# Range bounds on VectorE, grouped transposes and a new order of the first steps in a fused attention and ReGLU kernel

## The chip, the cores and the metric

The kernel runs on one core of one Trainium2 chip. The metric is the device time of one execution in microseconds, as the median of several runs. The engines that matter are TensorE (PE in the profile: matrix products and transposes, results in PSUM), VectorE (DVE), ScalarE (ACT: exponentials, ReLU, copies), GpSimd (POOL: masks, casts, and the issue of the DMAs that convert to bf16) and SyncE (SP: the issue of the other DMAs).

## What is computed

Causal attention with 16 beacon rows ahead of the sequence, then a gated feed-forward layer. B, H, S, Nb, D = 8, 8, 576, 16, 64; d_model = 512, d_ff = 1536, so 4608 tokens pass the second part.

```
k_all = concat([beacon_k, k], axis=2); v_all = concat([beacon_v, v], axis=2)
scores = (q @ k_all.T) / sqrt(D)            # beacon columns always visible
scores = where(causal, -1e9, scores)
a = exp(scores - scores.max(-1)); a /= a.sum(-1) + 1e-09
x = (a @ v_all), heads side by side         # 4608 x 512
out = (maximum(x @ w_gate, 0) * (x @ w_val)) @ w_out
```

## The kernel before

**Attention.** For each batch b the kernel holds `kT` and `qT` (d on the partitions, two heads in 128 partitions) and `v`. Scores are made transposed, keys on the partitions, in units: a unit is one PSUM tile `s` of two banks (L333, `Unit.qk`), one exponential on ScalarE into `e` (L341, `Unit.exp`) and, where the unit touches the diagonal, a mask on GpSimd (L349). The exponentials are not shifted by the row maximum. A chunk is a group g of four heads and a range of 240, 256 or 80 query columns (`CHUNKS`). When all units of a chunk are there, `Chunk.av` (L377) multiplies by v (`ab`) and by ones (`os`, the row sums); `invert` (L385) takes the reciprocal `r` of the sums on VectorE, `scale` (L390) writes `xT` = `ab` * `r`. The tiles `ab` and `os` have one buffer each; in batch 0 the chunks of group 1 take the two buffers of `f` instead.

**Range check.** Since no maximum is subtracted, `note` (L393 on) keeps track of r over all chunks: on GpSimd it turns "r below 1e-10" into 1e30 (`low`, L398) and adds r and `low` to a running sum `far` (L401, twice). Near the end VectorE reduces `far` (`rows_in_range`), a matmul counts the good rows, and a general path, not taken here, would run if a row were out of range. One note is kept back for the next step (`while len(notes) > 1`). The tile r has four buffers.

**Feed-forward.** Tokens are taken in tiles of 512 columns of `xT`. `Ffn.up` (L415 gate, ReLU on ScalarE L418, L421 value, product `hT` on VectorE L423) runs for each of the 12 blocks of d_ff; `Ffn.down` (L428) makes 128 rows of output, copied by ScalarE (L431) and stored by SP. Every PSUM result of this part is one of the two buffers of `f`.

**Order.** Everything is issued in the order of a step list, `plan`, and every engine runs its own instructions in that order. A step of a batch makes the scores of two units, does the `av`, `invert` of the chunks that came due, then some feed-forward groups (`mine`), with the `scale` behind the first of them, then the actions that were put at or behind this step (`at`, `after`), then notes. A batch has 7 steps. Batch 0 (steps 0 to 6) has no feed-forward work; four steps without attention (`ALONE`, 7 to 10) follow, then batch 1 (11 to 17), and from step 18 on the other batches. The third number of a plan entry is a quota of feed-forward work in us, kept as a credit (1.7 for an up, 2.6 for a down).

**Loading.** Batches 0 and 1 come as halves of 256 rows. Batch 0's are loaded in float32 by SP and cast on VectorE or ScalarE (`cast_half`), batch 1's are converted by GpSimd's DMA (`load_cast_half`, L267). `turn_half` (L273 on, transposes at L281, moves at L282) transposes a half on TensorE into a PSUM tile: 8 transposes, a move of these to `kT` or `qT`, 8 more, a second move. `turn_two` does this for the k and the q half with one `s` tile. The last 64 rows (`tails`) and the beacon rows go through `cast_rows` (L295) and `turn_rows` (L302, L303). The weights come by GpSimd's DMA (`load_w` L309, `load_wo` L314). Later batches are loaded by SP, cast on GpSimd (L246, L242) and transposed by DMA.

Of the kernel before, what the change touches and what calls it, by code (L numbers as in the profile page):

```python
# [153 lines left out]
def kernel(  # L154
# [12 lines left out]
    nc = tc.nc  # L167
# [26 lines left out]
    far = const.tile([P, 256], FP32, name="far")  # L194
    nc.gpsimd.memset(far, 0.0)
# [6 lines left out]
    nrm = main.enter_context(tc.tile_pool(name="nrm", bufs=4))  # L202
# [6 lines left out]
    class Batch:  # L209
# [60 lines left out]
        def turn_half(self, x, i, ps, moves):  # L270

            h = self.h.pop((x, i, "half"))
            dst, c0 = (self.qT, 0) if x == "q" else (self.kT, Nb)  # L273
            c0 += i * 256
            for g, move in enumerate(moves):
                js = slice(2 * g, 2 * g + 2)
                for r in range(2):
                    for j in (2 * g, 2 * g + 1):
                        for a in range(2):
                            c = ((2 * j + a) * 2 + r) * D  # L280
                            nc.tensor.transpose(ps[a * D:(a + 1) * D, j, r], h[:, c:c + D], ident)  # L281
                move(dst[:, js, c0:c0 + 256].rearrange("a j (p r) -> a j p r", r=2),  # L282
                     ps[:, js].rearrange("a j r p -> a j p r"))
# [70 lines left out]
    class Chunk:  # L354
# [39 lines left out]
        def note(self):  # L394

            n = CHUNKS[self.ci][1]
            low = nrm.tile([P, 256], FP32, name="low", bufs=1)
            nc.gpsimd.tensor_scalar(out=low[:, :n], in0=self.r[:, :n], scalar1=1e-10,  # L398
                                    scalar2=1e30, op0=ALU.is_lt, op1=ALU.mult)
            for x in (self.r, low):  # L400
                nc.gpsimd.tensor_tensor(out=far[:, :n], in0=far[:, :n], in1=x[:, :n], op=ALU.add)  # L401
# [38 lines left out]
    def rows_in_range():  # L440
        most = const.tile([P, 1], FP32, name="most")
        nc.vector.tensor_reduce(most, far, op=ALU.max, axis=AX.X)
        ok = const.tile([P, 1], BF16, name="ok")
        nc.vector.tensor_scalar(out=ok, in0=most, scalar1=1e10, scalar2=None, op0=ALU.is_le)
        return ok

    def count_rows(ok):
# [12 lines left out]
    plan = ([(0, i, 0.0) for i in range(STEPS)]  # L460
            + [(None, 0, 4.5)] * ALONE
            + [(1, i, 2.1) for i in range(STEPS)]
# [3 lines left out]
    with tc.manual_schedule():  # L466
# [7 lines left out]
        def at(step, action):  # L474
            later.setdefault(step, []).append(action)
# [7 lines left out]
        def load_rest(x):  # L483
            x.tails = [x.load_rows(k[x.b, :, 512:]), x.load_rows(q[x.b, :, 512:])]
            for t in range(NKT):
                x.load("v", t)
# [6 lines left out]
        ps = s_ps.tile([P, 2, NP, 2, P], BF16, name="s")  # L493
        first.cast_half("k", 0, dve)
        first.turn_half("k", 0, ps[:, 0], (dve, dve))
        first.cast_half("q", 0, act)
        first.turn_half("q", 0, ps[:, 1], (act, dve))
# [3 lines left out]
        def load_both(n0, n1):  # L501
            load_w(wg, moe_w_gate, n0, n1)
            load_w(wv, moe_w_val, n0, n1)

        def turn_two(x, i):
            ps = s_ps.tile([P, 2, NP, 2, P], BF16, name="s")
# [10 lines left out]
        later_half = {}  # L517

        def after(step, action):
            later_half.setdefault(step, []).append(action)  # L520
# [18 lines left out]
        after(5, lambda: second.load_cast_half("k", 1))  # L539
        after(5, lambda: second.load_cast_half("q", 1))  # L540
        after(6, lambda: load_wo(0, 6))
        after(6, lambda: load_wo(6, 12))
# [40 lines left out]
        for s, (b, i, quota) in enumerate(plan):  # L583
# [14 lines left out]
            for u in units:  # L598
                u.qk()
            if units:  # L600
                units[0].exp()
# [5 lines left out]
            mine = []  # L607
            while queue and credit > queue[0][1] / 2:
                mine.append(queue.pop(0))
                credit -= mine[-1][1]  # L610
# [24 lines left out]
            while len(notes) > 1:  # L635
                notes.pop(0)()
# [9 lines left out]
        for note in notes:  # L646
            note()
# [44 lines left out]
```

## Time and profile before

| | |
|---|---|
| median of 3 runs | 428.46 us (427.62 to 428.52) |
| profiled execution | 428.95 us, of which the span of its instructions is 427.2 us |
| TensorE busy | 388.0 us, 91% |
| VectorE busy | 175.1 us, 41% |
| ScalarE busy | 192.3 us, 45% |
| GpSimd busy | 218.5 us, 51% |
| mean granted TensorE clock | 0.97 |

The groups of the three lines of `note` on GpSimd hold 41.0, 28.3 and 28.3 us in 48 instructions each. A line of the timeline reads: start, duration, engine, source line, operation, output<-input with partitions x elements, count, and in brackets how long the engine had been idle and which instruction released it. A group line reads: line, engine, operation, output<-input, count | busy us, mean ns of one | idle time before. A line of the stages reads: stretch, its length, busy us (and instructions) of PE, PEld (TensorE's weight loads), DVE, ACT and POOL, mean granted TensorE clock, DMA share, GB/s.

### The profile page before, as it was taken

The page shows a single profiled execution, that of the slowest core. Times are in us where ns is not written, and L with a number is a line of the kernel's source. Part 1 is how long each engine was busy: PE and PEld are TensorE (multiplying, and loading weights), DVE is VectorE, ACT ScalarE, POOL GpSimd, SP SyncE. Part 2 cuts the span into 40 slices and gives each one's busy share as a digit, 9 for nine tenths or more (in the row PEclk, how much of TensorE's full clock was granted, in tenths as well). Part 3 has the DMA queues.
Part 4 walks back from the last instruction along what each step waited for, and adds up shares of the span by engine and source line. Part 5 has one row for each costly group of instructions (what it writes and reads, how often), then busy time and mean ns, then how long its engine had stood idle before and what let it go on. Part 6 is the DMA issues. An engine that isn't in the chain of part 4 may idle for free.

```text
span 427.2 us, 10264 instructions
## 1 busy us (share of the span) xinstructions
PE 388.0 (91%) x4265; PEld 189.2 (44%) x4265; DVE 175.1 (41%) x230; ACT 192.3 (45%) x267; POOL 218.5 (51%) x357
## 2 busy tenths in 40 slices
PE   2672877889999999999999999999999999999994
PEld 1342333445454545544554445444544454444441
DVE  2363243444454355434553455344534442411310
ACT  2561122564645465545545554555545533323221
POOL 1699810796658575756675576648551651000000
PEclk9997688899999999999999999999999999999999
DMA  8999994562993499359937993898110011001002
GB/s 216 194 211 196 187 187 80 112 117 74 203 185 60 134 205 171 69 131 204 168 60 152 191 161 57 175 195 144 46 69 0 5 51 49 2 25 74 2 26 79
DMA packets 146516, 49.85 MB, mean 117 GB/s; under 512 B 133152, under 2 KB 141856, under 8 KB 146464
## 3 DMA queue, kind: packets, MB, share of 16 engines
q1 hardware_dynamic: 137472, 43.37, 51.5%
q0 software_dynamic: 8992, 5.77, 9.3%
q8 instruction: 35, 0.57, 0.6%
q14 instruction: 17, 0.14, 0.1%
HBM read 38.27 MB, written 9.44 MB: 112 GB/s over the span
## 4 chain that ended last, share of the span: by engine, by line
PE 85%; POOL 7%; DVE 2%; DMA 2%; ACT 1%; SPq 1%; issue 1%; DVEq 0%; ACTq 0%; POOLq 0%
PE f L421 24%; PE f L415 24%; PE f L428 22%; PE ab L377 6%; PE s L333 6%; PE os L377 2%; POOL e L349 1%; DMA raw<-in_v_dram 1%; POOL wg L309 1%; POOL wv L309 1%; DMA wide<-in_k_dram 1%; POOL far L401 1%; POOL hwide L267 1%; POOL low L398 1%; POOL v L242 1%
## 5 line engine op out<-in xcount | busy, mean ns | idle before, releaser
L423 DVE TENSOR_TENSOR hT<-g,f 128x512 bf16<-128x512 f32 x108 | 74.2, 687 | 124.5 <-PE f L421 123.0
L341 ACT ACTIVATE e<-s 128x1024 bf16<-128x1024 f32 (+2 forms) x112 | 104.9, 964 | 25.8 <-PE s L333 25.0
L415 PE MATMUL f<-xT,wg 128*128 128x512 bf16 x432 | 115.5, 391 | 0.8 <-DVE r L385 0.8
L421 PE MATMUL f<-xT,wv 128*128 128x512 bf16 x432 | 113.1, 384 | 0.0
L418 ACT ACTIVATE g<-f 128x512 f32<-128x512 f32 x108 | 64.5, 597 | 108.0 <-PE f L415 107.9
L385 DVE RECIPROCAL r<-os 128x240 f32<-128x240 f32 (+2 forms) x45 | 61.1, 1358 | 90.9 <-PE os L377 86.7
L428 PE MATMUL f<-wo,hT 128*128 128x512 bf16 x432 | 97.3, 379 | 0.0
L349 POOL TENSOR_SCALAR_AFFINE_SELECT e<-e 128x512 bf16<-128x512 bf16 (+2 forms) x80 | 46.6, 593 | 94.2 <-ACT e L341 91.1
L421 PEld LDWEIGHTS <-wv 128*128 128x128 bf16 x432 | 42.6, 99 | 64.0 <-issue 22.9
L428 PEld LDWEIGHTS <-hT 128*128 128x128 bf16 x432 | 40.9, 98 | 48.7 <-issue 0.2
L415 PEld LDWEIGHTS <-wg 128*128 128x128 bf16 x432 | 40.2, 100 | 48.9 <-issue 5.0
L431 ACT COPY ob<-f 128x512 f32<-128x512 f32 x36 | 21.1, 585 | 75.6 <-PE f L428 63.4
L377 PE MATMUL ab<-e,v 128*32 128x80 bf16 (+4 forms) x1320 | 40.3, 236 | 6.4 <-POOL e L349 2.9
L246 POOL CAST half<-raw 128x512 bf16<-128x512 f32 (+2 forms) x60 | 35.8, 611 | 15.6 <-DMA raw<-in_k_dram 9.8
L398 POOL TENSOR_SCALAR low<-r 128x240 f32<-128x240 f32 (+2 forms) x48 | 41.0, 854 | 3.6
L333 PE MATMUL s<-qT,kT 64*128 64x80 bf16 (+3 forms) x704 | 36.7, 238 | 3.0 <-ACT e L341 2.2
L377 PEld LDWEIGHTS <-v 128*32 128x32 bf16 (+1 forms) x1408 | 27.4, 99 | 22.2 <-issue 11.7
L333 PEld LDWEIGHTS <-kT 64*128 64x128 bf16 x704 | 21.5, 98 | 26.6 <-issue 25.3
L242 POOL CAST v<-raw 128x512 bf16<-128x512 f32 (+1 forms) x40 | 25.5, 642 | 14.5 <-DMA raw<-in_v_dram 13.9
L377 PE MATMUL os<-e,ones 128*32 128x240 bf16 (+4 forms) x660 | 32.6, 234 | 0.0
L401 POOL TENSOR_TENSOR far<-far,low 128x240 f32<-128x240 f32 (+2 forms) x48 | 28.3, 589 | 3.8
L401 POOL TENSOR_TENSOR far<-far,r 128x240 f32<-128x240 f32 (+2 forms) x48 | 28.3, 590 | 3.1
(40 smaller groups left out, 111.7 us busy)
## 6 DMA issues: line engine op xcount, KB each, us to landing
out_dram<-ob SPq DMA_DIRECT2D x36, 256.0 KB, 2.4
raw<-in_v_dram SPq DMA_DIRECT2D x24, 256.0 KB, 5.0
raw<-in_q_dram SPq DMA_DIRECT2D x24, 256.0 KB, 5.0
raw<-in_k_dram SPq DMA_DIRECT2D x18, 256.0 KB, 4.3
raw<-in_v_dram SPq DMA_DIRECT2D x8, 224.0 KB, 5.3
wo<-in_moe_w_out_dram POOLq DMA_DIRECT2D x2, 768.0 KB, 11.6
raw<-in_k_dram SPq DMA_DIRECT2D x6, 224.0 KB, 4.5
raw<-in_v_dram SPq DMA_DIRECT2D x8, 160.0 KB, 4.3
```

Source lines behind the costliest of these rows:

```text
L333: nc.tensor.matmul(self.s[:, a, c + j * n:c + (j + 1) * n], self.batch.kT[rows, 2 * g + j, kt * P:(kt + 1) * P], self.batch.qT[rows, 2 * g ...
L341: nc.scalar.activation(e[:, :k * 4 * n].rearrange("p (k a x) -> p a k x", k=k, a=2), self.s[:, :, :k * 2 * n].rearrange("p a (k x) -> p a ...
L349: nc.gpsimd.affine_select(out=cols[:, :, :m], in_=cols[:, :, :m], pattern=[[0, 4], [1, m]], compare_op=ALU.is_ge, fill=0.0, base=base, cha ...
L377: nc.tensor.matmul(o[:, q0 - cq0:q0 - cq0 + n], w, e[:kr, 2 * (hh % 2) + hh // 2], start=(i == 0 and part != 1), stop=(i == self.last), sk ...
L385: nc.vector.reciprocal(self.r[:, :n], self.os[:, :n])
L398: nc.gpsimd.tensor_scalar(out=low[:, :n], in0=self.r[:, :n], scalar1=1e-10, scalar2=1e30, op0=ALU.is_lt, op1=ALU.mult)
L401: nc.gpsimd.tensor_tensor(out=far[:, :n], in0=far[:, :n], in1=x[:, :n], op=ALU.add)
L415: nc.tensor.matmul(g[:, :n], wg[:, ki, nf * P:(nf + 1) * P], x[:, ki], start=(ki == 0), stop=(ki == KM - 1))
L418: nc.scalar.activation(gs[:, :n], g[:, :n], AF.Relu)
L421: nc.tensor.matmul(u[:, :n], wv[:, ki, nf * P:(nf + 1) * P], x[:, ki], start=(ki == 0), stop=(ki == KM - 1))
L423: nc.vector.tensor_mul(self.h[:, nf, c0:c1], gs[:, :n], u[:, :n])
L428: nc.tensor.matmul(o, self.h[:, nf, ms * P:(ms + 1) * P], wo[:, nf, :], start=(nf == 0), stop=(nf == NF - 1))
```

## The change

1. `note` no longer runs on GpSimd: VectorE keeps two running tiles, `least` and `most`, by one `min` and one `max` with r (both operands float32 in SBUF). A note is issued at the end of its own step, none is kept back. The tile r has three buffers in place of four. `rows_in_range` compares both tiles and reduces.
2. `turn_half` issues all 16 transposes of a half, then its two moves. Each half now has a PSUM tile of its own: batch 0's are `f` tiles, batch 1's are two `s` tiles where there was one.
3. Batch 0: the k half 1 is turned after step 0, the q half 1 between the two score units of step 1 (`between`); the tails are cast on VectorE in step 1, where ScalarE cast them in step 0. SP loads the first three tiles of v ahead of the tails.
4. Later actions move by one step: the last weight columns from step 2 to 3, the halves of batch 1 from 4 and 5 to 5 and 6, `wo` from 6 to 7.
5. In `plan`, whole numbers now count feed-forward groups instead of microseconds: 0, 3, 3, 2 in the four steps alone and 1 in each step of batch 1.

```diff
-    far = const.tile([P, 256], FP32, name="far")
-    nc.gpsimd.memset(far, 0.0)
+    bounds = [const.tile([P, 256], FP32, name=n) for n in ("least", "most")]
+    for x in bounds:
+        nc.vector.memset(x, 1.0)
...
-    nrm = main.enter_context(tc.tile_pool(name="nrm", bufs=4))
+    nrm = main.enter_context(tc.tile_pool(name="nrm", bufs=3))
...
+            for j in range(NP):
+                for r in range(2):
+                    for a in range(2):
+                        c = ((2 * j + a) * 2 + r) * D
+                        nc.tensor.transpose(ps[a * D:(a + 1) * D, j, r], h[:, c:c + D], ident)
             for g, move in enumerate(moves):
                 js = slice(2 * g, 2 * g + 2)
-                for r in range(2):
-                    for j in (2 * g, 2 * g + 1):
-                        for a in range(2):
-                            c = ((2 * j + a) * 2 + r) * D
-                            nc.tensor.transpose(ps[a * D:(a + 1) * D, j, r], h[:, c:c + D], ident)
...
         def note(self):
             n = CHUNKS[self.ci][1]
-            low = nrm.tile([P, 256], FP32, name="low", bufs=1)
-            nc.gpsimd.tensor_scalar(out=low[:, :n], in0=self.r[:, :n], scalar1=1e-10,
-                                    scalar2=1e30, op0=ALU.is_lt, op1=ALU.mult)
-            for x in (self.r, low):
-                nc.gpsimd.tensor_tensor(out=far[:, :n], in0=far[:, :n], in1=x[:, :n], op=ALU.add)
+            for x, op in zip(bounds, (ALU.min, ALU.max)):
+                nc.vector.tensor_tensor(out=x[:, :n], in0=x[:, :n], in1=self.r[:, :n], op=op)
...
+        nc.vector.tensor_scalar(out=least, in0=least, scalar1=1e-10, scalar2=None, op0=ALU.is_ge)
+        nc.vector.scalar_tensor_tensor(out=least, in0=most, scalar=1e10, in1=least,
+                                       op0=ALU.is_le, op1=ALU.mult)
+        nc.vector.tensor_reduce(ok, least, op=ALU.min, axis=AX.X)
...
-            + [(None, 0, 4.5)] * ALONE
-            + [(1, i, 2.1) for i in range(STEPS)]
+            + [(None, 0, n) for n in (0, 3, 3, 2)]
+            + [(1, i, 1) for i in range(STEPS)]
...
         def turn_two(x, i):
-            ps = s_ps.tile([P, 2, NP, 2, P], BF16, name="s")
-            for y, n in enumerate("kq"):
-                x.turn_half(n, i, ps[:, y], (dve, act))
+            for n in "kq":
+                ps = s_ps.tile([P, 2, NP, 2, P], BF16, name="s")
+                x.turn_half(n, i, ps[:, 0], (dve, act))
...
+        after(0, lambda: first.turn_half("k", 1, f_half(), (dve, act)))
         after(0, lambda: first.cast_half("q", 1, dve))
-        after(0, lambda: turn_two(first, 1))
         after(0, lambda: first.cast("v", 1, pool))
-        after(0, lambda: cast_tails(first, act))
-        at(1, lambda: turn_tails(first))
+        between[1] = lambda: first.turn_half("q", 1, f_half(), (dve, act))
+        at(1, lambda: None)
+        at(1, lambda: cast_tails(first, dve))
+        after(1, lambda: turn_tails(first))
...
-        after(2, lambda: load_both(768, 1536))
         after(3, lambda: first.cast("v", 4, pool))
+        after(3, lambda: load_both(768, 1536))
         after(4, lambda: load_rest(second))
-        after(4, lambda: second.load_cast_half("k", 0))
-        after(4, lambda: second.load_cast_half("q", 0))
...
+        after(5, lambda: second.load_cast_half("k", 0))
+        after(5, lambda: second.load_cast_half("q", 0))
...
-            while len(notes) > 1:
+            while notes:
                 notes.pop(0)()
```

**What moves on VectorE in batch 0.** The chunks (group 0 or 1, columns 256 or 80) of batch 0 in VectorE's order; `os`/`ab` are group 0, `f` group 1. Before:

```order
L385 RECIPROCAL r<-os 128x256
L390 TENSOR_TENSOR xT<-ab,r 128x2x256
L385 RECIPROCAL r<-f 128x256
L390 TENSOR_TENSOR xT<-f,r 128x2x256
L385 RECIPROCAL r<-os 128x80
L390 TENSOR_TENSOR xT<-ab,r 128x2x80
```

The same chunks with the change:

```order
L386 RECIPROCAL r<-os 128x256
L391 TENSOR_TENSOR xT<-ab,r 128x2x256
L398 TENSOR_TENSOR least<-least,r 128x256
L398 TENSOR_TENSOR most<-most,r 128x256
L386 RECIPROCAL r<-f 128x256
L391 TENSOR_TENSOR xT<-f,r 128x2x256
L398 TENSOR_TENSOR least<-least,r 128x256
L398 TENSOR_TENSOR most<-most,r 128x256
L386 RECIPROCAL r<-os 128x80
L391 TENSOR_TENSOR xT<-ab,r 128x2x80
```

A `min` and a `max` now stand between a chunk's `xT` and the next chunk's reciprocal.

**What moves on GpSimd in batch 0**, steps 3 to 6: masks (AFFINE_SELECT), notes and DMA issues. Before:

```order
L398 TENSOR_SCALAR low<-r 128x240
L401 TENSOR_TENSOR far<-far,r 128x240
L401 TENSOR_TENSOR far<-far,low 128x240
L349 AFFINE_SELECT e<-e 128x4x128
L242 CAST v<-raw 80x512
L267 DMA hwide<-in_k_dram 128x8x128
L267 DMA hwide<-in_q_dram 128x8x128
L398 TENSOR_SCALAR low<-r 128x240
L401 TENSOR_TENSOR far<-far,r 128x240
L401 TENSOR_TENSOR far<-far,low 128x240
L349 AFFINE_SELECT e<-e 128x320
```

With the change:

```order
L350 AFFINE_SELECT e<-e 128x4x128
L243 CAST v<-raw 80x512
L310 DMA wg<-in_moe_w_gate_dram 128x2x768 x2
L310 DMA wv<-in_moe_w_val_dram 128x2x768 x2
L350 AFFINE_SELECT e<-e 128x320
L268 DMA hwide<-in_k_dram 128x8x128
L268 DMA hwide<-in_q_dram 128x8x128
L350 AFFINE_SELECT e<-e 128x320
```

The notes are gone ahead of each mask; the last weight columns are issued behind the mask of step 3, and the halves of batch 1 behind the first 320-wide mask.

**What moves on VectorE around the tails**, steps 1 and 2 of batch 0 (`half` 64x512 are the tails, `kT<-f` and `qT<-f` their moves). Before:

```order
L282 COPY qT<-s 128x2x256
L385 RECIPROCAL r<-os 128x240
L390 TENSOR_TENSOR xT<-ab,r 128x2x240
L303 COPY kT<-f 128x4x64
L303 COPY qT<-f 128x4x64
L385 RECIPROCAL r<-f 128x240
```

With the change:

```order
L283 COPY qT<-f 128x2x256
L386 RECIPROCAL r<-os 128x240
L391 TENSOR_TENSOR xT<-ab,r 128x2x240
L296 CAST half<-raw 64x512 x2
L304 COPY kT<-f 128x4x64
L304 COPY qT<-f 128x4x64
L398 TENSOR_TENSOR least<-least,r 128x240
L398 TENSOR_TENSOR most<-most,r 128x240
L386 RECIPROCAL r<-f 128x240
```

The casts of the tails stand on VectorE behind the first chunk's `xT`; on TensorE their transposes stand, as before, ahead of the scores of step 2.

More of the change, by code (lines that the diff above doesn't have):

```diff
@@ L440, in rows_in_range @@
     def rows_in_range():
[L441 to L442 removed]
+        least, most = bounds
         ok = const.tile([P, 1], BF16, name="ok")
[L444 removed]
+        nc.vector.tensor_scalar(out=least, in0=least, scalar1=1e-10, scalar2=None, op0=ALU.is_ge)
+        nc.vector.scalar_tensor_tensor(out=least, in0=most, scalar=1e10, in1=least,
+                                       op0=ALU.is_le, op1=ALU.mult)
+        nc.vector.tensor_reduce(ok, least, op=ALU.min, axis=AX.X)
         return ok
@@ L483, in load_rest @@
         def load_rest(x):
+            for t in range(3):
+                x.load("v", t)
             x.tails = [x.load_rows(k[x.b, :, 512:]), x.load_rows(q[x.b, :, 512:])]
-            for t in range(NKT):
+            for t in range(3, NKT):
                 x.load("v", t)
@@ L597 @@
                 units = [Unit(batches[b], order[2 * i + x]) for x in range(2)]
-            for u in units:
+            for j, u in enumerate(units):
                 u.qk()
+                if j == 0 and s in between:
+                    between[s]()
             if units:
```

23 lines of the change are left out of this document (12 added, 11 removed).

## The prediction

> **What bounds the kernel now.** I read the page's clock row first, then the busy times by stage, then the timeline of the stages where TensorE is not full.
>
> ```profile
> PEclk9997688899999999999999999999999999999999
> ```
>
> ```profile
> 30.00:44.40 14.40, 4.70 (x208) 3.77 (x209) 6.55 (x8) 3.13 (x4) 13.81 (x19) 0.72 1.35 199
> 44.40:56.40 12.00, 12.00 (x41) 4.54 (x41) 4.06 (x8) 2.98 (x5) 7.23 (x13) 0.76 1.31 199
> 56.40:61.70 5.30, 2.32 (x45) 1.73 (x44) 2.64 (x6) 0.59 (x1) 1.86 (x3) 0.87 0.87 165
> 61.70:69.90 8.20, 8.20 (x28) 2.98 (x28) 1.37 (x2) 2.38 (x4) 0.00 (x0) 0.67 0.88 157
> 69.90:75.30 5.40, 2.61 (x45) 1.65 (x44) 1.98 (x3) 1.73 (x3) 0.00 (x0) 0.88 0.00 0
> 75.30:103.10 27.80, 24.65 (x350) 12.51 (x348) 13.08 (x14) 15.14 (x20) 22.48 (x36) 0.96 0.52 100
> 103.10:421.00 317.90, 317.84 (x3338) 151.93 (x3337) 134.30 (x173) 151.17 (x213) 156.16 (x256) 1.00 0.52 104
> ```
>
> From 103.1 us TensorE is busy without a break at full clock (317.84 of 317.90). The change leaves its amount of work alone: eight ups in the four steps alone, four ups and three downs in batch 1, in both versions. So the time moves by what the first 103 us gain or lose, unless VectorE's new work opens gaps later. GpSimd is nearly full from 30 to 44.4 us (13.81 of 14.40) while TensorE has 4.70. The timeline shows who waits:
>
> ```profile
> 37.06 0.69 POOL L401 TENSOR_TENSOR far<-far,low 128x240 f32<-128x240 f32 x1
> 37.70 0.48 POOL L349 TENSOR_SCALAR_AFFINE_SELECT e<-e 128x320 bf16<-128x320 bf16 x1
> 38.23 0.32 PE L377 MATMUL ab<-e,v 80*32 80x80 bf16 x8 [2.88 <-POOL e L349]
> 41.98 0.72 POOL L401 TENSOR_TENSOR far<-far,low 128x256 f32<-128x256 f32 x1
> 42.66 0.47 POOL L349 TENSOR_SCALAR_AFFINE_SELECT e<-e 128x320 bf16<-128x320 bf16 x1
> 43.18 0.33 PE L377 MATMUL f<-e,v 80*32 80x80 bf16 x8 [3.76 <-POOL e L349]
> 44.40 1.86 PE L415 MATMUL f<-xT,wg 128*128 128x512 bf16 x4 [0.83 <-DVE r L385]
> ```
>
> Masks stand behind notes; TensorE waits 2.88 and 3.76 us for them, and the first up begins at 44.40. Later it waits inside the turns of batch 1's halves, each time for a move, before the next eight transposes:
>
> ```profile
> 57.60 0.41 PE L281 MATMUL s<-ident,hwide 128*64 128x128 bf16 x8
> 58.81 0.41 PE L281 MATMUL s<-ident,hwide 128*64 128x128 bf16 x8 [0.79 <-DVE kT L282]
> 61.16 0.64 PE L281 MATMUL s<-ident,hwide 128*64 128x128 bf16 x8 [0.85 <-DVE qT L282]
> 75.33 1.89 PE L415 MATMUL f<-xT,wg 128*128 128x512 bf16 x4
> ```
>
> After such gaps the clock is down: a group of four 512-column products takes twice as long.
>
> ```profile
> 46.27 1.71 PE f L421 x4
> 50.82 0.86 PE f L415 x4
> ```
>
> **The change, part by part.** Prices of one instruction in ns (after the bar: busy us, mean ns of one):
>
> ```profile
> L385 DVE RECIPROCAL r<-os 128x256 f32<-128x256 f32 x15 | 26.4, 1758 | 33.6 <-PE os L377 33.6
> L385 DVE RECIPROCAL r<-os 128x80 f32<-128x80 f32 x15 | 9.9, 658 | 26.4 <-PE os L377 26.4
> L390 DVE TENSOR_TENSOR xT<-ab,r 128x512 bf16<-128x512 f32 x15 | 10.3, 688 | 0.3
> L390 DVE TENSOR_TENSOR xT<-ab,r 128x160 bf16<-128x160 f32 x15 | 4.8, 322 | 0.3
> L401 POOL TENSOR_TENSOR far<-far,r 128x256 f32<-128x256 f32 x16 | 11.6, 726 | 1.0
> L349 POOL TENSOR_SCALAR_AFFINE_SELECT e<-e 128x512 bf16<-128x512 bf16 x48 | 29.7, 635 | 10.4 <-ACT e L341 7.3 <-DMA out_dram<-ob 1.7 <-DMA raw<-in_q_dram 0.7
> L282 DVE COPY kT<-s 128x512 bf16<-128x512 bf16 x5 | 3.4, 690 | 1.7 <-PE s L281 1.7
> L282 ACT COPY kT<-s 128x512 bf16<-128x512 bf16 x3 | 1.8, 585 | 6.6 <-PE s L281 6.6
> L295 DVE CAST half<-raw 64x512 bf16<-64x512 f32 x2 | 0.7, 407 | 0.0
> L195 POOL MEMSET far<- 128x256 f32 x1 | 0.3, 316 | 0.0
> L442 DVE TENSOR_REDUCE most<-far 128x1 f32<-128x256 f32 x1 | 0.4, 410 | 0.0
> ```
>
> No row shows min or max. VectorE's two-input rows grow by (688 - 322) / 352 = 1.04 ns an element, so 256 columns make 0.42 us and 80 make 0.24, a pair 0.84 and 0.48. One operand of those rows lies in PSUM, here both lie in SBUF; below, an instruction costs at least half (0.2), above, GpSimd's own row of that shape (0.73). I take 0.42, by VectorE's rows, which are the nearest.
>
> *Up to the first up.* I follow the chain in the new order from these rows.
>
> ```profile
> 18.94 1.87 ACT L341 ACTIVATE e<-s 128x960 bf16<-128x960 f32 x2
> 20.96 1.66 DVE L385 RECIPROCAL r<-os 128x240 f32<-128x240 f32 x1 [4.27 <-PE os L377]
> 21.91 1.94 ACT L341 ACTIVATE e<-s 128x1024 bf16<-128x1024 f32 x2 [1.10 <-PE s L333]
> 30.06 1.76 DVE L385 RECIPROCAL r<-os 128x256 f32<-128x256 f32 x1 [2.98 <-PE os L377]
> ```
>
> Step 1's exponentials start about 1.8 us earlier (near 17.1): two waits between transposes go, and ScalarE no longer casts the tails first. The first chunk's reciprocal follows at about 19.8, 1.2 earlier. Then part is given back: xT ends at 19.8 + 1.66 + 0.66 = 22.1, two tail casts of 0.41 follow on VectorE (22.9), and TensorE, whose order has the tails' transposes ahead of step 2's scores, waits for them: step 2's exponentials start at about 23.9, 2.0 late. ScalarE then runs without the gaps that it had, so that the reciprocal of the first 256-column chunk comes at about 30.5, 0.45 late. From there VectorE sets the pace: 30.5 + 1.76 + 0.69 + 0.84 = 33.8 for the first chunk with its pair, 1.76 + 0.69 for the second (36.25), which frees the `f` tile of the last chunk's av; the pair 0.84, the 80-column chunk 0.66 + 0.32 + 0.48, and the last one's 0.66 + 0.32 end at 39.5. The masks are no longer late: with no notes ahead of them, GpSimd's weight issues and hwide issues end before TensorE reaches them. On SP the tails now stand behind three tiles of v: they land later, but VectorE takes them only at 22.1, and the first tile of v comes sooner. One buffer less of r costs nothing, since VectorE alone now writes and reads it, in its own order. Hand-offs of 0.1 to 0.2 make it 39.7, so **-4.7 us**, with bounds of 2 (step 2 later, a pair at 1.46) and 6.5 (a pair at 0.4, no tail wait).
>
> *From the first up to the end of the eighth.* Before: 12.0 + 5.3 + 8.2 = 25.5. Now six ups come first: 12.0 for five with the clock down at first, as before, and 1.9 for the sixth. The small transposes take 1.2 (56.4 to 57.6), the two halves 4 x 0.41 = 1.6 without waits, because each has its own tile; the moves run under the seventh up. Two warm ups and a ReLU that stands behind ScalarE's moves: 3.8. Together 20.5, **-5.0 us**; of these 2.5 are the waits and 2.5 the slow clock of the sixth and seventh up in the row of 61.7 (0.67).
>
> *To the ninth up.* Before 5.4. Now 1.6 of transposes, and the first scores wait for their `s` tile: two moves 0.69 + 0.59 behind the k half, the same behind the q half on the same engines: 3.5, **-1.9 us**.
>
> *Batch 1.* Before 27.8, with 24.65 busy, of which the ninth up's slow start costs 0.9. The longest gap is this one, in a step that had no feed-forward group; now each step has one:
>
> ```profile
> 95.36 0.40 PE L377 MATMUL ab<-e,v 128*32 128x256 bf16 x8 [1.64 <-DVE xT L390]
> ```
>
> I take 2.0 of the 3.15 us idle and the 0.9: **-2.9 us** (between 1 and 4).
>
> *From batch 2 on.* 36 pairs on VectorE. Its room between two jobs there:
>
> ```profile
> 157.76 0.69 DVE L423 TENSOR_TENSOR hT<-g,f 128x512 bf16<-128x512 f32 x1 [1.69 <-PE f L421]
> 161.50 0.69 DVE L423 TENSOR_TENSOR hT<-g,f 128x512 bf16<-128x512 f32 x1 [1.18 <-PE f L421]
> 163.24 1.76 DVE L385 RECIPROCAL r<-os 128x256 f32<-128x256 f32 x1 [1.05 <-PE os L377]
> ```
>
> A pair stands behind the last hT of a step; the next job is idle for 1.05 us (a reciprocal) or 1.69 (an hT) before it, and 0.84 fits into either. The loop value product, hT, value product is tight, so whatever overruns costs TensorE at once; I charge 0.3 in all. The two memsets (316 ns on GpSimd) lie before the first load lands, 0.6 if they did not; the reduction at the end (410 now, two more instructions of about 0.4) fits into the 1.18 beside an hT, or costs 0.8.
>
> Sum: -4.7 - 5.0 - 1.9 - 2.9 + 0.3 = -14.2. The profiled execution took 428.95 (a span of 427.2 and 1.75 around it), 0.49 over the median: 414.75 for such an execution, 414.3 against the median of 428.46.
>
> **The rivals.** *The clock stays up before the first up* (gaps of 1 to 2 us in place of 2.88 and 3.76): three groups at 0.86 in place of 1.71 save 2.6 more, 411.7. Against it: VectorE's chain leaves TensorE little work from 34 to 39.7.
>
> *The clock falls in the turn.* 2.8 us of transposes in a row may count as idleness; the two ups behind them then run slow, +2.6, 416.9. For it: in the stage from 56.4 the clock fell with 45 short instructions in it (0.87 on the mean). Against it: half of that stage was waiting. The Trainium skill (TensorE: Matmul & The Clock Gate, Part 4) says that transposes do not count as activity for the clock; no run here shows dense transposes alone.
>
> *The data come too late.* The DMA moves 199 GB/s to 56.4 us, before as after, and the last weight columns, with `wo` and the halves of batch 1 behind them in GpSimd's queue, are issued a step later, some 3 us by my chain. The halves themselves no longer wait for notes there, and are needed only at about 55. If the columns or batch 1's halves are not there, the turn waits and the 4.7 are lost: 419.0.
>
> *Slower: VectorE's pairs hold TensorE in the long stage.* If each min and max waits for a running mask of 0.64, a pair takes 0.84 + 1.28 = 2.1, 1.05 over the room; at the half of the 36 pairs whose overrun meets a full-length reciprocal or hT that is 18 x 1.05 = 19, so 433. It turns the sign from 0.39 us a pair over all 36 on. Against it: GpSimd loses its notes and is idle more than half of that stage. The Trainium skill (SBUF — State Buffer, Who interferes with whom) speaks for it: a VectorE instruction with two SBUF inputs contends with a GpSimd instruction that reads SBUF. This trace has no such VectorE instruction.
>
> *No change*: the start is paced by loads altogether and the ups only wait elsewhere, 428.
>
> **How the numbers follow.** Forecast 0.50, clock up 0.18, clock falls 0.14, data late 0.10, VectorE slower 0.05, no change 0.03. A measurement of this kernel tells about 0.2% from none. Faster 0.92, same 0.03, slower 0.05. The range goes from 410.5 (clock up, and 1 of the bounds) to 420.0 (data late, and 1).
>
> **What would show it.** Right: first up at 39.7, the ninth at about 63.7, no wait of TensorE for a mask over 1 us, no wait between the transposes of a half, batch 2 at about 89, and a stage behind it of the same length. Wrong: a later first up with TensorE waiting for a DMA; min and max well over 0.42; gaps of TensorE in the long stage ahead of value products, with a min or max on VectorE just before the hT that they wait for.

## The result and the profile after

The changed kernel takes 411.56 us (median of 4 runs, 410.49 to 412.26) beside 428.49 for the kernel before on the same chip: a ratio of 0.9603, 95% interval 0.9571 to 0.9635. The forecast was 414.3, the range 410.5 to 420.0. The profiled execution took 410.93 us, of which the span is 408.7. By the ratio 17.0 us are gained. In a later set of runs the unedited kernel gave 0.9605 (0.9577 to 0.9633).

The clock row of the page of after, then its stages (columns as in the table of before; the second stretch begins with the first up, the last with batch 2):

```profile
PEclk9998999999999999999999999999999999999999
```

```profile
30.00:38.23 8.23, 4.18 (x202) 3.33 (x197) 8.09 (x14) 3.13 (x4) 7.72 (x12) 1.00 1.14 206
38.23:50.97 12.74, 12.52 (x47) 4.96 (x47) 6.24 (x11) 3.58 (x6) 3.92 (x6) 0.87 1.48 183
50.97:57.25 6.28, 5.35 (x60) 2.92 (x61) 3.25 (x7) 2.27 (x4) 0.61 (x1) 1.00 1.22 203
57.25:60.38 3.13, 1.86 (x45) 1.50 (x46) 1.89 (x3) 1.62 (x3) 0.63 (x1) 1.00 1.00 221
60.38:86.12 25.74, 22.90 (x343) 12.07 (x348) 16.38 (x24) 15.11 (x20) 13.17 (x22) 1.00 0.82 149
86.12:403.00 316.88, 312.73 (x3290) 151.98 (x3337) 157.94 (x248) 151.82 (x213) 79.21 (x140) 1.00 0.44 105
```

Before the first up VectorE is now the full engine (8.09 of 8.23, GpSimd 7.72). Of before's five low digits in the clock row (76888) one is left (8). In the last row 48 matmul records fewer stand than in before's, so most of the 4.15 us between 312.73 and 316.88 is no sign of waiting; the view of waits lists 2.3 us there.

TensorE's timeline of after, at the first up and at the turn:

```profile
38.23 0.59 PE L412 MATMUL f<-xT,wg 128*128 128x512 bf16 x1 [2.29 <-DVE r L386]
...
39.89 1.88 PE L418 MATMUL f<-xT,wv 128*128 128x512 bf16 x4
41.60 1.03 PE L412 MATMUL f<-xT,wg 128*128 128x512 bf16 x4
...
52.30 1.08 PE L280 MATMUL s<-ident,hwide 128*64 128x128 bf16 x32
...
57.25 1.08 PE L280 MATMUL s<-ident,hwide 128*64 128x128 bf16 x32
59.38 0.38 PE L334 MATMUL s<-qT,kT 64*128 64x240 bf16 x4 [1.05 <-ACT kT L283]
```

The first up begins at 38.23 (44.40 before). Only its gate and value group run at half clock; the next group takes 1.03. All 32 transposes of a turn run in 1.08 us without a wait.

VectorE's chain just ahead of the first up, in after:

```profile
32.44 0.42 DVE L398 TENSOR_TENSOR most<-most,r 128x256 f32<-128x256 f32 x1
32.77 1.75 DVE L386 RECIPROCAL r<-f 128x256 f32<-128x256 f32 x1
...
36.51 0.33 DVE L391 TENSOR_TENSOR xT<-ab,r 128x160 bf16<-128x160 f32 x1
36.75 0.27 DVE L398 TENSOR_TENSOR least<-least,r 128x80 f32<-128x80 f32 x1
36.95 0.67 DVE L398 TENSOR_TENSOR most<-most,r 128x80 f32<-128x80 f32 x1
37.54 0.64 DVE L386 RECIPROCAL r<-f 128x80 f32<-128x80 f32 x1
```

VectorE doesn't idle between these rows, nor in the four left out: the reciprocals, `xT` and the pairs stand end to end up to 38.23.

Four marks make every trace below comparable: A, the start of the first up; B, from there to the first scores of batch 1 (turns and ups); C, from there to the first scores of batch 2; D, the rest of the span. D is as exact as the spans, 0.1 us. "Slow" counts, in B, the groups of four 512-column products at about half clock, as the timeline shows them.

| kernel (one trace each) | A | B | C | D | span | slow |
|---|---|---|---|---|---|---|
| before | 44.40 | 29.65 | 29.09 | 324.06 | 427.2 | 6.5 |
| b_notes | 37.52 | 29.48 | 29.01 | 323.49 | 419.5 | 6 |
| b_turns | 44.54 | 21.18 | 29.50 | 324.18 | 419.4 | 2 |
| b_notes_turns | 38.68 | 21.73 | 29.43 | 323.56 | 413.4 | 3 |
| a_gpnotes | 42.28 | 21.90 | 26.74 | 322.88 | 413.8 | 3 |
| a_oldplan | 39.44 | 21.79 | 29.44 | 324.43 | 415.1 | 3 |
| after | 38.23 | 21.15 | 26.74 | 322.58 | 408.7 | 2 |
| a_again (after, unedited) | 39.04 | 21.19 | 26.74 | 323.23 | 410.2 | 2 |
| a_nonotes | 35.19 | 19.51 | 28.75 | 323.05 | 406.5 | 0 |
| a_double | 40.80 | 21.84 | 26.74 | 322.62 | 412.0 | 3 |
| a_tails_act | 35.42 | 21.12 | 27.29 | 322.87 | 406.7 | 2 |
| a_busy | 37.61 | 19.51 | 26.85 | 322.93 | 406.9 | 0 |
| a_tails_late | 33.72 | 23.86 | 27.35 | 323.27 | 408.2 | 2 |
| best | 35.02 | 23.54 | 26.74 | 323.20 | 408.5 | 2 |

### The profile page after: what moved, and what is told of

Same layout as the page of the kernel before. It is cut to its first block, busy times and chain, and to the rows that moved or that the text cites. A ratio compares the mean times of both kernels' runs of the same rounds, so it can differ in the third digit from the quotient of the medians.

```text
span 408.7 us, 10091 instructions
## 1 busy us (share of the span) xinstructions
PE 375.5 (92%) x4209; PEld 187.0 (46%) x4265; DVE 208.2 (51%) x331; ACT 191.6 (47%) x265; POOL 121.9 (30%) x212
## 4 chain that ended last, share of the span: by engine, by line
PE 86%; DVE 5%; ACT 2%; DMA 2%; issue 2%; POOL 1%; SPq 0%; DVEq 0%; ACTq 0%; POOLq 0%
PE f L418 25%; PE f L425 23%; PE f L412 22%; PE ab L378 7%; PE s L334 6%; PE os L378 3%; DVE r L386 2%; DVE hT L420 2%; DMA raw<-in_v_dram 1%; ACT e L342 1%; DMA wide<-in_k_dram 1%; DVE xT L391 1%; ACT g L415 1%; POOL e L350 0%; POOL wg L310 0%
## 5 line engine op out<-in xcount | busy, mean ns | idle before, releaser
L418 PE MATMUL f<-xT,wv 128*128 128x512 bf16 x428 | 110.9, 380 | 1.6 <-DVE hT L420 1.2
L412 PE MATMUL f<-xT,wg 128*128 128x512 bf16 x397 | 107.8, 382 | 4.1 <-DVE r L386 2.3
L425 PE MATMUL f<-wo,hT 128*128 128x512 bf16 x415 | 94.9, 379 | 1.9 <-issue 1.4
L247 POOL CAST half<-raw 128x512 bf16<-128x512 f32 (+2 forms) x60 | 36.9, 633 | 24.1 <-DMA raw<-in_q_dram 11.8
L391 DVE TENSOR_TENSOR xT<-ab,r 128x480 bf16<-128x480 f32 (+2 forms) x45 | 24.8, 552 | 0.7
L398 DVE TENSOR_TENSOR least<-least,r 128x240 f32<-128x240 f32 (+2 forms) x48 | 22.6, 471 | 0.0
L378 PEld LDWEIGHTS <-ones 128*32 128x32 bf16 (+1 forms) x704 | 19.6, 101 | 1.0 <-issue 0.6
```

The costliest lines, as they stand in the source:

```text
L247: copy(h[:n], raw[:n])
L378: nc.tensor.matmul(o[:, q0 - cq0:q0 - cq0 + n], w, e[:kr, 2 * (hh % 2) + hh // 2], start=(i == 0 and part != 1), stop=(i == self.last), sk ...
L391: nc.vector.tensor_mul(xT[:, 2 * self.g:2 * self.g + 2, t0:t0 + n], self.ab[:, :, :n], self.r[:, :n].unsqueeze(1).to_broadcast([P, 2, n]))
L412: nc.tensor.matmul(g[:, :n], wg[:, ki, nf * P:(nf + 1) * P], x[:, ki], start=(ki == 0), stop=(ki == KM - 1))
L418: nc.tensor.matmul(u[:, :n], wv[:, ki, nf * P:(nf + 1) * P], x[:, ki], start=(ki == 0), stop=(ki == KM - 1))
L425: nc.tensor.matmul(o, self.h[:, nf, ms * P:(ms + 1) * P], wo[:, nf, :], start=(nf == 0), stop=(nf == NF - 1))
```

## The experiments

Three theories were on record. **M**, the prediction's: the time is made before batch 2 by separate waits (masks behind notes, moves inside the turns, a step without feed-forward), and the pairs of min and max are hidden later. **V**: moving the notes is worth little, since VectorE becomes the chain. **C**: most of the gain is the clock. The first four runs shared one chip and its runs of before (429.64), the next four another set (428.50), the last four a third (429.31).

### One part at a time, upward from before

**b_notes**: before with item 1 of the change alone.

```diff
-                nc.gpsimd.tensor_tensor(out=far[:, :n], in0=far[:, :n], in1=x[:, :n], op=ALU.add)
+                nc.vector.tensor_tensor(out=x[:, :n], in0=x[:, :n], in1=self.r[:, :n], op=op)
...
-            while len(notes) > 1:
+            while notes:
```

> The kernel before with one part of the change: the range bounds kept by VectorE's min and max, nothing else moved. Theory M (the time is made in the first 87 us, by several separate waits, and the masks that stood behind GpSimd's bounds are one of them): about 423.5 us, 421 to 425.5, since the first up comes some 4 to 5 us earlier and nothing later changes. Rival V (VectorE already sets the pace to the first up, so that some 2.2 us of min and max there take back what GpSimd gives): 427.5 or more. Rival C (most of the gain is the clock, which follows the gaps of TensorE): 426 or more, with the clock at half speed in the same windows after the first up as before.

Measured: 421.67, ratio 0.983 (0.9804 to 0.9856). The timeline of b_notes at the first up:

```profile
37.52 0.59 PE L412 MATMUL f<-xT,wg 128*128 128x512 bf16 x1 [1.75 <-DVE r L386]
39.17 1.91 PE L418 MATMUL f<-xT,wv 128*128 128x512 bf16 x4
```

GpSimd's masks, in the same trace, have no note ahead of them:

```profile
32.19 0.62 POOL L350 TENSOR_SCALAR_AFFINE_SELECT e<-e 128x320 bf16<-128x320 bf16 x1
34.55 0.51 POOL L350 TENSOR_SCALAR_AFFINE_SELECT e<-e 128x320 bf16<-128x320 bf16 x1
```

The first up is 6.9 us earlier, more than M had, and everything behind keeps its length (B, C and D within 0.6 of before's). V falls. So does C for this part: the clock is down in B as before, as C had it, and the 7.3 us came all the same.

**b_turns**: before with the grouped transposes alone, a PSUM tile to each half, in the order before.

```diff
+            for j in range(NP):
+                for r in range(2):
+                    for a in range(2):
+                        c = ((2 * j + a) * 2 + r) * D
+                        nc.tensor.transpose(ps[a * D:(a + 1) * D, j, r], h[:, c:c + D], ident)
...
-            ps = s_ps.tile([P, 2, NP, 2, P], BF16, name="s")
-            for y, n in enumerate("kq"):
-                x.turn_half(n, i, ps[:, y], (dve, act))
+            for n in "kq":
+                ps = s_ps.tile([P, 2, NP, 2, P], BF16, name="s")
+                x.turn_half(n, i, ps[:, 0], (dve, act))
```

> The kernel before with one part of the change: in the two turns all 16 transposes of a half go ahead of its two moves, into a tile of their own; bounds still on GpSimd, order of the first steps as it was. M: about 421.5 us, 419 to 424: the waits for the moves inside the turns (about 2.5 us in one and 1.9 in the other) go, and some of the slow clock behind them. V expects most of the whole gain here: 417 or less. C: the waits alone, about 424, unless the windows at half clock go too; if they go, 418.

Measured: 422.01, ratio 0.9834 (0.9811 to 0.9856). B falls by 8.5 us and A doesn't move (44.54). In batch 0 grouping brings step 1's exponentials forward (15.68, before 18.94), but step 2's start as before (22.07, before 21.91), and the masks still set the first up. Of the 8.5, 7.5 lie behind the start of the first turn; 1.0 lies ahead of it, where the clock is down for some 1.5 groups fewer. The timeline of b_turns at the turn:

```profile
56.76 1.08 PE L279 MATMUL s<-ident,hwide 128*64 128x128 bf16 x32
57.78 1.04 PE L415 MATMUL f<-xT,wg 128*128 128x512 bf16 x3
63.59 1.08 PE L279 MATMUL s<-ident,hwide 128*64 128x128 bf16 x32
```

The ups behind the turn run at full clock (1.04, where before had 1.89). Some 6.5 groups ran slow in before's B and about 2 here; at 0.85 each (1.71 against 0.86) that is about 4 us, 2.6 of them behind the turn, and the rest of the 8.5 goes with the waits between the transposes. This is M's mechanism, with the clock nearly as large a share as the waits; so C is right for nearly half of this part.

**b_notes_turns**: the edits of the two kernels above together.

> The kernel before with both of these parts; what is left of the change is the order of the first steps and the new counts. M: the two add up, about 416.5 us, 414 to 419, so that some 5 us remain for the order and the counts. V: no faster than with the turns alone. C: more than the sum of the two, since the gaps that go together take whole windows of half clock away: 414 or less.

Measured: 415.50, ratio 0.969 (0.9662 to 0.9717). The two parts alone give 7.3 and 7.1 by their ratios, both 13.3: they nearly add up. C's surplus does not appear. What is left of the change is worth 3.7 (0.969 against 0.9603).

### One part taken back, downward from after

**a_gpnotes**: after with `far` and `low` on GpSimd again, as before the change.

```diff
-                nc.vector.tensor_tensor(out=x[:, :n], in0=x[:, :n], in1=self.r[:, :n], op=op)
+                nc.gpsimd.tensor_tensor(out=far[:, :n], in0=far[:, :n], in1=x[:, :n], op=ALU.add)
```

> The changed kernel with the range bounds given back to GpSimd in the form they had before. M: about 416.5 us, 414.5 to 418.5: the masks of the first steps stand behind the bounds again and the first up comes 4 to 5 us later. V: 411.5 or faster, VectorE's chain being shorter by some 2 us. C: slower by whole windows of 3.4 us at half clock, half of each lost: 413 to 415.

Measured: 415.47, ratio 0.9674 (0.9651 to 0.9697): 3.0 us over after, with the first up 3.2 to 4.1 later (42.28). GpSimd's row in a_gpnotes shows the old pattern, a sum ahead of a mask:

```profile
39.86 0.72 POOL L401 TENSOR_TENSOR far<-far,low 128x256 f32<-128x256 f32 x1
40.54 0.48 POOL L349 TENSOR_SCALAR_AFFINE_SELECT e<-e 128x320 bf16<-128x320 bf16 x1
```

TensorE waits 4.23 us for that mask. V falls again. Against before's 428.5 the ratio makes 414.5, which lies in C's range and at the lower end of M's; the trace is on M's side, as the first up is late behind a mask and only one more group runs slow (3 against 2, 0.85 us). But the notes are worth 7.3 alone and 3.0 here: with them on GpSimd the new order itself brings the first up forward (44.40 or 44.54 to 42.28); with them on VectorE it doesn't (38.68 to 38.23, 39.04 and 39.44). The parts overlap.

These four first ups scatter for a reason of their own: the pair ahead of the last reciprocal takes 0.94 us in after, 2.06 in a_oldplan, 2.22 in b_notes_turns and 2.53 in a_again, where it takes 0.46 in b_notes. Without what goes beyond 0.46 the four would lie between 36.9 and 37.8 (an estimate from these rows), so that no gain of the order was hidden by it.

**a_oldplan**: after with the old counts.

```diff
-            + [(None, 0, n) for n in (0, 3, 3, 2)]
-            + [(1, i, 1) for i in range(STEPS)]
+            + [(None, 0, 4.5)] * ALONE
+            + [(1, i, 2.1) for i in range(STEPS)]
```

> The changed kernel with the old counts of feed-forward groups for the first steps. M: 1 to 2 us slower than the changed kernel's 411.56 (ratio to before about 0.964), since one step of batch 1 is again without a group and waits 1.6 us for xT; the later steps only pass their groups on. V and C: no difference, within 0.3.

Measured: 415.92, ratio 0.9689 (0.9658 to 0.9719), 3.7 over after by the ratios (4.4 by the medians): more than M had, and V and C are wrong. The timeline of a_oldplan in batch 1 has the old gap again:

```profile
81.26 0.40 PE L378 MATMUL ab<-e,v 128*32 128x256 bf16 x8 [1.56 <-DVE xT L391]
```

C is 29.0 to 29.5 in the five traces with the old counts and 26.74 in after: 2.3 to 2.8 us. D differs too: 323.5 to 324.4 in the five traces with the old counts, 322.6 to 323.3 in the nine with the new ones, no overlap, 1.0 between the means. And a_oldplan stands where b_notes_turns stands (0.9689 and 0.969): the new order of the first steps, without the counts, is worth nothing that these runs could tell (each interval reaches 1.2 or 1.3 us to either side) once the notes are on VectorE.

### What the pairs cost

**a_nonotes**: after without range bounds; `least` and `most` keep their starting values, so the check of the range is left out.

```diff
         def note(self):
+            return
```

> The changed kernel with no range bounds at all (the min and max of every chunk are left out, so that the last output is not computed). It gives what the min and max still cost: M: 1.8 to 2.2 us in VectorE's chain to the first up (two pairs of 0.84 and one of 0.48 there) and 0 to 1.2 in the long stage, so 408.4 to 409.8, ratio 0.953 to 0.956. V: 4 us or more faster. C: as M for the first up, and another 1.7 if the clock's slow window at the first up goes with the shorter gap.

Measured: 410.01, ratio 0.9574 (0.9537 to 0.9611). The first up is 3.0 to 3.9 us earlier and no group runs slow; the wait ahead of the first up in a_nonotes is short:

```profile
35.19 1.02 PE L410 MATMUL f<-xT,wg 128*128 128x512 bf16 x4 [0.84 <-DVE r L386]
```

Yet by the ratios only about 1.2 us arrive at the end, and the intervals overlap. One reason is that C is 2.0 longer. The other is the clock: the traced execution (408.29) is one of three with a mean granted clock of 0.994 to 0.998 and 408.0 to 408.6 us; the other three have 0.987 to 0.989 and 411.4 to 412.2. TensorE and GpSimd in a_nonotes, in batch 1's first step:

```profile
61.03 0.30 PE L378 MATMUL ab<-e,v 128*32 128x128 bf16 x8 [1.54 <-POOL e L350]
```

```profile
57.78 0.64 POOL L243 CAST v<-raw 128x512 bf16<-128x512 f32 x1 [6.17 <-DMA raw<-in_v_dram]
58.37 0.58 POOL L350 TENSOR_SCALAR_AFFINE_SELECT e<-e 128x448 bf16<-128x448 bf16 x1
60.35 1.22 POOL L350 TENSOR_SCALAR_AFFINE_SELECT e<-e 128x512 bf16<-128x512 bf16 x2
```

The first mask of batch 1 stands on GpSimd behind a cast of v that waits 6.17 us for its load, and the masks behind it come late too. So a late load is a real limit, though not of the weight columns or the halves, which the prediction's rival named. In after GpSimd idles 1.96 us between that cast and the first mask: the limit lies about 2 us further on than the change goes.

**a_double**: after with each min and max twice.

```diff
-            for x, op in zip(bounds, (ALU.min, ALU.max)):
+            for x, op in 2 * tuple(zip(bounds, (ALU.min, ALU.max))):
```

> The changed kernel with every min and max issued twice (the second changes nothing in the result). A pair becomes 1.68 us where VectorE's room in the long stage was 1.05 to 1.69. M, by the prediction's account of the room: 2.0 to 2.2 us more up to the first up, and 0.63 at up to half of the 36 later pairs, so between 413.7 and 425. If the room is wider than that account has it (TensorE waits for hT for 1.2 us in all now), only the 2 us: 413.7. V: 425 or more.

Measured: 413.47, ratio 0.9649 (0.9624 to 0.9673), 1.9 over after. The first up comes at 40.80, and D is 322.62, as in after. From the first scores of batch 2 to the last scores of all it takes 241.06 us, to the hundredth as after and a_nonotes. So even a pair of 1.68 fits in the long stage; the 1.05 that the prediction called the room was idle time ahead of a reciprocal, and evidently a later reciprocal is not at once a wait of TensorE.

### What comes next

**a_tails_act**: after with the tails cast by ScalarE.

```diff
-        at(1, lambda: cast_tails(first, dve))
+        at(1, lambda: cast_tails(first, act))
```

> The changed kernel with the two casts of the tails on ScalarE, which waits 5.10 us there, in place of VectorE, where they stand behind the first xT. M: step 2's exponentials start 2 to 2.5 us earlier than 22.68 and the first up some 1.5 to 2 earlier than 39.04, 409.5 to 410, if ScalarE's exponentials and not VectorE's chain decide; if VectorE's chain from the reciprocal of the first 256-column chunk decides (it is busy 8.90 of 9.04 us), that chain starts earlier too and keeps 1 or more of it. V: 0, since VectorE's chain keeps its length.

Measured: 409.28, ratio 0.9557 (0.9528 to 0.9586). ScalarE in after:

```profile
15.69 1.89 ACT L342 ACTIVATE e<-s 128x960 bf16<-128x960 f32 x2
22.68 5.78 ACT L342 ACTIVATE e<-s 128x1024 bf16<-128x1024 f32 x6 [5.10 <-PE s L334]
```

and in a_tails_act:

```profile
15.71 1.89 ACT L342 ACTIVATE e<-s 128x960 bf16<-128x960 f32 x2
17.47 1.13 ACT L296 CAST half<-raw 64x512 bf16<-64x512 f32 x2
19.52 1.94 ACT L342 ACTIVATE e<-s 128x1024 bf16<-128x1024 f32 x2 [0.92 <-PE s L334]
```

In after ScalarE is done with step 1 early and then idles 5.10 us, because the transposes of the tails wait on TensorE for casts that VectorE makes behind the first `xT`. On ScalarE the casts fill that hole, step 2's exponentials start 3.2 earlier and the first up 2.8, and V's 0 is wrong. Some 0.5 of the 2.8 comes from the pair ahead of the last reciprocal, which takes 0.46 here and 0.94 in after. With the old order b_notes_turns starts step 1's exponentials at 15.09 and step 2's at 20.24 (after 15.69 and 22.68): step 1 owes its early start to the grouped transposes, and what the new order could have gained in step 2 it gave away with the casts.

**a_busy**: after with twelve unused products ahead of the first up.

```diff
+            if s == 7:
+                pad = s_ps.tile([P, 2, 512], FP32, name="s")
+                for d in range(12):
+                    nc.tensor.matmul(pad[:, d % 2], first.kT[:, 0, :P], first.qT[:, 0, :512],
+                                     start=True, stop=True)
```

> The changed kernel with twelve unused 128x512 products ahead of its first up, where TensorE waits 2.29 us for a reciprocal. C: the clock stays up through the first ups, no group of four products takes 1.9 us, and 1.5 to 1.7 us are saved: 410 (ratio to before about 0.9565). M: the same up to 0.4 us, since the twelve products may run over the gap's end. If the clock of the first ups doesn't depend on this gap: 411.5 to 412, with the same one or two slow groups.

Measured: 410.71, ratio 0.9573 (0.9543 to 0.9604), beside 0.9605 for a_again in the same set. The timeline of a_busy:

```profile
35.01 2.76 PE L616 MATMUL s<-qT,kT 128*128 128x512 bf16 x11
37.61 1.03 PE L412 MATMUL f<-xT,wg 128*128 128x512 bf16 x4
38.48 1.03 PE L418 MATMUL f<-xT,wv 128*128 128x512 bf16 x4
```

No group is slow and B is 1.64 shorter. The mean granted clock of the six executions is 0.993 to 0.999, beside 0.989 to 0.993 in a_again's six: how busy TensorE is ahead of the first up does set the clock behind it. By the medians 1.1 us arrive, and the two intervals overlap.

**a_tails_late** and **best**: a_tails_act's edit, and the pairs of batch 0 held back until step 8, with eight buffers of r in place of three; `best` adds eight products as in a_busy.

```diff
-    nrm = main.enter_context(tc.tile_pool(name="nrm", bufs=3))
+    nrm = main.enter_context(tc.tile_pool(name="nrm", bufs=8))
...
-            while notes:
+            while notes and not 1 <= s <= 7:
```

> The changed kernel with the casts of the tails on ScalarE and with the min and max of batch 0's first steps held back until step 8, still computing all outputs. The two edits apart moved the first up from 38.2 to 35.4 and (with no bounds at all) to 35.2. If VectorE's chain alone sets the start, M: first up at 32.5 to 33.5, about 407 (ratio 0.950). If the loads set the next limit, D: the first up comes as early, but batch 1's first masks wait for a cast of v whose load lands at about 57.5 in the runs so far, so that 2 to 3.5 us are given back between the turns and batch 2: 409 to 410, no faster than with the tails alone (0.9557).

> As the kernel before it in this list, with eight unused 128x512 products ahead of the first up as well. M and C: 1 to 1.7 us faster than without them if there are slow groups there, 405.5 (ratio 0.946). D: the same as without them, 409 to 410, since the loads of batch 1 set the time.

Measured: 410.11 (0.9561, 0.9531 to 0.9592) and 410.04 (0.9565, 0.9534 to 0.9595); a_again gave 411.77. D stands here for the theory of late loads, not for the mark. The first up of a_tails_late comes at 33.72, nearly as early as both theories had it, but the loss is not where the theory of late loads put it: C is only 0.6 longer than after's (27.35), and B is 2.7 longer. VectorE in a_tails_late:

```profile
41.07 0.39 DVE L398 TENSOR_TENSOR least<-least,r 128x240 f32<-128x240 f32 x1
...
43.84 0.67 DVE L398 TENSOR_TENSOR most<-most,r 128x80 f32<-128x80 f32 x1
44.43 0.64 DVE L398 TENSOR_TENSOR least<-least,r 128x80 f32<-128x80 f32 x1
44.99 0.23 DVE L398 TENSOR_TENSOR most<-most,r 128x80 f32<-128x80 f32 x1
45.15 1.27 DVE L420 TENSOR_TENSOR hT<-g,f 128x512 bf16<-128x512 f32 x2
```

and TensorE:

```profile
45.87 1.87 PE L412 MATMUL f<-xT,wg 128*128 128x512 bf16 x4 [2.08 <-DVE hT L420]
47.53 1.78 PE L418 MATMUL f<-xT,wv 128*128 128x512 bf16 x4
```

The twelve held-back instructions come in one block of 4.1 us, an `hT` stands behind it, TensorE waits 2.08 us, and the two groups behind the wait run at half clock on top. No group is slow at the first up of a_tails_late, so the products of best had nothing to save there. The number of the late loads was met for another reason, so these two kernels do not tell whether the loads would have set the limit. The fastest of all by its median ratio is a_tails_act, a one-word edit; its interval overlaps those of a_busy, a_tails_late and best.

## Why the prediction was right, and which terms were off

Faster, by the mechanism named: four of the five terms have the forecast's sign. They are measured from the two traces, in the prediction's own stages. Before's traced execution lies 0.5 above its median and after's 0.6 below, so the sum comes out larger than the 17.0 of the ratio:

- **To the first up**, -6.2 (38.23) where -4.7 was forecast. b_notes alone gives -6.9, so the masks behind the notes were the whole of it, as said; from 20 us on after's waits list none for a mask, where before's list 8.2 us. The mis-sized term is the start of step 1: its exponentials were forecast 1.8 earlier and came 3.25 earlier (15.69), and b_turns shows that the grouped transposes alone make this (15.68). So step 2's exponentials came at 22.68 in place of 23.9, and the reciprocal of the first 256-column chunk at 29.70 in place of 30.5, 0.8 of the 1.5 us. The cause given for the delay of step 2, the tails behind `xT`, is shown by a_tails_act. The price of the 80-column pair was wrong the other way: 0.94 and 2.53 in the two traces where 0.48 was forecast, and in the second of these the first up comes at 39.04.
- **First up to the end of the eighth**, -6.5 (38.23 to 57.25, 19.0) where -5.0 was forecast. "The clock down at first, as before" was the mis-sized term: two slow groups in place of some three and a half, about 1.2 us. The rival that the clock stays up was half right; a_busy shows its other half.
- **To the ninth up**, -2.3 against -1.9. The transposes took 1.08 where 1.6 was charged; the scores' wait for the moves is there (1.05).
- **Batch 1**, -2.1 against -2.9. The 2.0 for the step without a group held: a_oldplan brings it back. The 0.9 for the ninth up's slow start did not: in b_turns that up runs at full clock and C is no shorter.
- **From batch 2 on**, -1.5 against +0.3, the one wrong sign. The pairs cost nothing there (a_double, a_nonotes). Some 0.5 of it is the end behind the last downs (16.2 against 16.7), which scatters from 16.2 to 16.9 over all traces. The rest goes with the new counts: from the first scores of batch 2 to the last scores of all it takes 241.8 to 242.2 us in the five traces with the old counts and 241.0 to 241.4 in the nine with the new. In TensorE's rows the batches of after repeat every 41.35 us where before's take 41.48 (and one 38.89); why the counts of the first steps do that isn't settled, as no wait in the trace of before accounts for it.

These make -18.6, the spans' difference -18.5, against -14.2 forecast. The parts by the ratios: notes 7.3 alone, turns 6.0 on top of them, counts 3.7, the order of the first steps nothing; together the 17.0.

**VectorE's pairs hold TensorE** (the slower rival) did not happen in the long stage: TensorE waits there for `hT` 1.2 us in all, 0.2 at most at a time. The contention behind it is real, though. Groups of min and max in after (mean ns behind the bar's first number):

```profile
L398 DVE TENSOR_TENSOR least<-least,r 128x80 f32<-128x80 f32 x16 | 8.7, 545 | 0.0
L398 DVE TENSOR_TENSOR most<-most,r 128x80 f32<-128x80 f32 x16 | 5.2, 322 | 0.0
L398 DVE TENSOR_TENSOR least<-least,r 128x256 f32<-128x256 f32 x16 | 6.6, 415 | 0.0
L398 DVE TENSOR_TENSOR most<-most,r 128x256 f32<-128x256 f32 x16 | 6.7, 418 | 0.0
```

At 256 columns the forecast's 0.42 is met. At 80 the means are 2.4 and 1.4 times the 0.23 of an undisturbed one, and one instance in a_again lies on the chain to the first up, just as GpSimd casts v:

```profile
36.30 2.11 DVE L398 TENSOR_TENSOR most<-most,r 128x80 f32<-128x80 f32 x1
38.34 0.65 DVE L386 RECIPROCAL r<-f 128x80 f32<-128x80 f32 x1
```

```profile
36.50 2.40 POOL L243 CAST v<-raw 128x512 bf16<-128x512 f32 x4
```

The rule of the Trainium skill (SBUF — State Buffer, Who interferes with whom), that a VectorE instruction with two SBUF inputs contends with a GpSimd instruction that reads SBUF, agrees with these rows. Its price on the chain to the first up is up to 1.9 us for one instruction, in a_again (2.11), and nearly that in b_notes_turns (1.97); the same program's first up comes at 38.23 in one trace and at 39.04 in the other, where the `most` ahead of the last reciprocal takes 0.67 in the one and 2.11 in the other. So the slower rival had the mechanism right and the stage wrong.

**The clock falls in the turn** did not happen: the ups behind both turns run at full clock (1.02 to 1.04 a group), in after and in b_turns. A turn is only 1.08 us of transposes, not the 2.8 in a row that the rival feared, so this leaves the rule of the Trainium skill (TensorE: Matmul & The Clock Gate, Part 4), that a transpose doesn't count as activity of TensorE in the same way, untested.

## What to carry to other kernels

Look at what an in-order queue holds ahead of a short instruction that another engine needs: here bookkeeping of 2.4 us stood ahead of masks of 0.5, and moving it was worth more than its own cost on the new engine. When several waits of one start-up chain are cut at once, price each alone and expect the worth of a part to depend on the others (the new order brought the first up 2 us forward with the notes on GpSimd and not at all with them on VectorE). The next limit lies close behind: in these runs what was gained further at the first up was partly given back, to masks behind the cast of a late load or to deferred work that came all at once.

## What the runs showed of the hardware that was not expected

- A 128x80 min or max takes 0.23 us undisturbed and up to 2.11 us while GpSimd casts; the cast is stretched as well, in a_tails_late to 3.53 us for a tile of 80 rows whose like takes 0.62 in after:

```profile
40.87 3.53 POOL L243 CAST v<-raw 80x512 bf16<-80x512 f32 x1 [1.09 <-DMA raw<-in_v_dram]
```

- How busy TensorE is ahead of the first up goes with the clock behind it. In the 10 us ahead of it TensorE is busy 1.8 to 6.4 us in the ten traces that have slow groups there, and 7.4 to 8.7 us in the four that have none (a_nonotes, a_busy, a_tails_late, best). The last gap alone doesn't decide: it is 2.29 us in after with two slow groups and 0.84 in a_nonotes with none, but 0.83 in before, b_turns and a_gpnotes, which have two to three and a half slow groups and a wait of 3.8 to 4.2 us just ahead of it. This sorts 14 traces and is no measured threshold. The same kernel may fall on either side, as the two groups of times and clocks of a_nonotes suggest; only one of its six executions has a trace.
